# One DMA transpose for a unit's inner rows, and the last 32 rows by one TensorE transpose and one store

## The chip, the cores and the metric

The kernel runs on one core of a Trainium2 chip. The metric is the device time of one execution in microseconds (us); the time before is the median of three runs. Engines are named as the profile names them: PE is TensorE (PEld its weight loads), ACT is ScalarE, DVE is VectorE, POOL is GpSimd, SP is SyncE, which here only issues DMAs. "SPq", "ACTq" and "POOLq" are the instruction queues of those engines.

## The reference

A convolution over the sequence with three taps, a batch normalisation and SiLU, in bf16:

```python
B, S, C, K = 2, 2048, 1024, 3          # x: (B, S, C), w: (K, C, C)
xp = jnp.pad(x, ((0, 0), (1, 1), (0, 0)))
y = sum(jnp.einsum('bsc,cd->bsd', xp[:, k:k + S, :], w[k]) for k in range(K))
y = (y - mean) * (g / jnp.sqrt(var + 1e-5)) + b
return silu(y)
```

## The kernel before, in words

The three taps are done by a short-convolution transform: six neighbouring output positions (`R = 6`) form a block, and eight products (`NJ = 8`) give all six. 2048 positions make `NB = 342` blocks, of which the last holds only two real positions. `T_sb` holds the transformed input; the transformed weights `u` and a few untransformed ones (`wch`) are the stationary operands.

The work is cut into 16 units: `dc` (128 of the 1024 output channels) times `bi` (batch). Unit 14 is the last `dc` with batch 0, unit 15 the last `dc` with batch 1. A unit is 64 matmuls of 342 columns (8 products of 8 channel tiles, line 324), DVE combinations (line 342) and SiLUs on ACT (line 347). The SiLUs write `yT`, one tile for each batch, laid out as [channel, row i of the block, block]; the rows i go from 0 to 5. "Inner" rows are 1 to 4, "outer" ones 0 and 5. Then the data are turned to [block, row, channel] in a tile `o` and stored, so that each block's rows are rows of the output.

How the end of one unit lies inside the next: `Unit.run` takes a list of pairs (place, function) and calls the functions at the places 1 to 6 (`behind(n)`) of its own order of products. `rest` supplies three of them for the unit before: `silu_inner`, `last` (product 7 into row 5, then its SiLU) and `first` (product 0 into row 0, then its SiLU). During units 13 and 14 `silu_inner` and `last` stand at place 4 and `first` at place 5, between product (2,5) and product (2,6). The order on all engines is the program order; nothing is rearranged.

Units 0 to 13 are turned by a DMA transpose (`turn`, line 458), issued on SP after the next unit's `run`: one for all six rows, for unit 13 two (rows 1 to 5, row 0). They are stored one unit later by `store`: blocks 0 to 127, 128 to 255 and 256 to 335 (three DMAs, line 471), blocks 336 to 340 (one, line 471) and the two last positions (one, line 475). For units 12 and 13 the two small ones are issued on POOL (`late`).

Unit 15 is computed in two parts: `h0` (blocks 128 to 341) and `h1` (blocks 0 to 127). Unit 14 and unit 15 are turned on PE (`put`: transposes of 128x128 against `ident`, line 429, a copy out of PSUM, line 430, stores, line 435). Unit 14's inner rows of block groups 0 and 1 are put at place 5 of `h0.run` (8 transposes, a DVE copy), its outer rows at place 2 of `h1.run` (6 transposes, an ACT copy), its inner rows of group 2 at place 3 of `h1.run` (4 transposes, an ACT copy). `put_rest` stores its last six blocks with two DMAs on POOL (lines 446 and 450). Unit 15's stores go to SP and ACT, its `put_rest` to POOL.

Of the kernel before, what the change touches and what calls it, by code (L numbers as in the profile page):

```python
# [11 lines left out]
BF16 = mybir.dt.bfloat16  # L12
# [3 lines left out]
P = 128  # L16
R = 6
# [9 lines left out]
def kernel(  # L27
# [10 lines left out]
    nc = tc.nc  # L38
    B, S, C = x.shape
    D = w.shape[2]  # L40
    CT, DC = C // P, D // P
    NB = -(-S // R)
# [22 lines left out]
    ps = pspool.tile([P, 8, 512], FP32, name="ps")  # L65
    T_sb = [tpool.tile([P, CT, NJ, NB], BF16, name=f"T_sb{bi}") for bi in range(B)]

    rows = consts.tile([4 * DC, P], BF16, name="rows")
# [65 lines left out]
    def load_w(pair, k, half=None):  # L134

        if (pair, "tile") not in raw:
            raw[pair, "tile"] = wpools[pair % 2].tile([P, 3, CT, 2, P], BF16, name=f"wch{pair % 2}")
        wch = raw[pair, "tile"]
        h0, h1 = (0, 2) if half is None else (half, half + 1)
        cols = slice((2 * pair + h0) * P, (2 * pair + h1) * P)  # L140
        nc.sync.dma_start(  # L141
            out=wch[:, k, :, h0:h1].rearrange("p c h d -> p c (h d)"), in_=w_all[:, k, :, cols]
        )
        clock["dma"] += 1200.0 * (h1 - h0)
        for h in range(2):
            raw[2 * pair + h] = wch[:, :, :, h]
# [77 lines left out]
    ident = consts.tile([P, P], BF16, name="ident")  # L224
# [68 lines left out]
    NK = -(-NB // P)  # L293
    NBP = NK * P
    assert S % R
    yts = [ypool.tile([P, R, NBP], BF16, name=f"yT{q}") for q in range(B)]
    for t in yts:
        nc.gpsimd.memset(t[:, :, NB:NBP], 0.0)

    class Unit:  # L300
# [117 lines left out]

        def put(self, o, rows, bank, evac, queues, blocks=None):

            i0, i1 = min(rows), max(rows)
            every = slice(i0, i1 + 1, 1 if i1 == i0 else (i1 - i0) // (len(rows) - 1))
            blocks = blocks or range(self.lo // P, -(-self.hi // P))
            n = min(self.hi - self.lo, P)
            v = ps[:, bank].bitcast(BF16)[0:n, 0:len(rows) * len(blocks) * P]
            v = v.rearrange("p (i k d) -> p i k d", i=len(rows), k=len(blocks))
            for a, i in enumerate(rows):
                for q, k in enumerate(blocks):
                    nc.tensor.transpose(v[:, a, q], self.yT[:, i, k * P:k * P + n], ident)  # L429
            evac(o[0:n, every, blocks[0]:blocks[-1] + 1], v)  # L430
            outs = out[self.bi, :, self.dc * P:(self.dc + 1) * P]
            full = S // R
            for q, k in zip(queues, blocks):
                hi = min((k + 1) * P, full // 16 * 16)
                q.dma_start(
                    out=outs[k * P * R:hi * R].rearrange("(p i) d -> p i d", i=R)[:, every],
                    in_=o[0:hi - k * P, every, k],
                )

        def put_rest(self, o, queue):  # L440

            full = S // R
            lo = full // 16 * 16
            k, p0 = lo // P, lo % P
            rows = out[self.bi, :, self.dc * P:(self.dc + 1) * P]
            queue.dma_start(  # L446
                out=rows[lo * R:full * R].rearrange("(p i) d -> p i d", i=R), in_=o[p0:p0 + full - lo, :, k]
            )
            k, p0 = full // P, full % P
            queue.dma_start(  # L450
                out=rows[full * R:S].rearrange("(p i) d -> p i d", p=1), in_=o[p0:p0 + 1, 0:S % R, k]
            )

        def turn(self, pool=opool, parts=((0, R),)):

# [4 lines left out]
                    in_=self.yT[:, lo:hi].rearrange("d i (k p) -> d (i k) p", p=P),  # L460
                )

        def store(self, queues=()):

            o, full = self.o, S // R
            rows = out[self.bi, :, self.dc * P:(self.dc + 1) * P]
            cuts = [k * P for k in range(full // P + 1)] + [full // 16 * 16, full]
            queues = list(queues) or [nc.sync] * len(cuts)
            for q, lo, hi in zip(queues, cuts, cuts[1:]):
                k, p0 = lo // P, lo % P  # L470
                q.dma_start(
                    out=rows[lo * R:hi * R].rearrange("(p i) d -> p i d", i=R), in_=o[p0:p0 + hi - lo, :, k]
                )
            k, p0 = full // P, full % P
            queues[-1].dma_start(
                out=rows[full * R:S].rearrange("(p i) d -> p i d", p=1), in_=o[p0:p0 + 1, 0:S % R, k]
            )

    for i, wi in enumerate(order):
        load_x(0, wi)  # L480
# [22 lines left out]
    class Between:  # L503


        n = done = cols = 0
# [16 lines left out]

    between = Between()
    seq = [(dc, bi) for dc in range(DC) for bi in range(B)]
    late = [nc.sync] * (S // R // P + 1) + [nc.gpsimd]
    before = prev = None
    for i, (dc, bi) in enumerate(seq[:-1]):
        unit = Unit(dc, bi, i % 2 * 4)
        unit.run(  # L530
            between, prev.rest(between, *((4, 5) if i >= len(seq) - 3 else (5, 6))) if prev else [(5, between.rest)],
            1 if i == 0 else 2 if i == 2 else dc + 2 if bi == 1 and 0 < dc < DC - 2 else None,
        )
        if i == 0:
            xwin_scope.close()
            olast = ctx.enter_context(tc.tile_pool(name="olast", bufs=3))
            wpools[1] = ctx.enter_context(tc.tile_pool(name="wpool1", bufs=1))
        if i in (0, 4, 8):
            for k in range(3):
                load_w(i // 4 + 1, k)  # L540
        if i == len(seq) - 2:
            prev.turn(olast, ((1, R), (0, 1)))
        elif prev:
            prev.turn()
        if before:
            before.store(late if i == len(seq) - 2 else ())
        before, prev = prev, unit
    before.store(late)
    dc, bi = seq[-1]
    sp, ac = nc.sync, nc.scalar  # L550
    inner, outer = tuple(range(1, R - 1)), (0, R - 1)
    to_v, to_s = nc.vector.tensor_copy, nc.scalar.copy
    o = olast.tile([P, R, NK, P], BF16, name="o")
    h0 = Unit(dc, bi, 4, P, NB)
    h0.run(between, prev.rest(between, 5, 5) + [(5, lambda: prev.put(o, inner, 1, to_v, (sp, sp), (0, 1)))])
    h1 = Unit(dc, bi, 0, 0, P)
    h1.run(between, [
        (2, lambda: prev.put(o, outer, 2, to_s, (sp, sp, sp))),
        (3, lambda: prev.put(o, inner, 1, to_s, (sp,), (2,))), (3, lambda: prev.put_rest(o, nc.gpsimd)),
    ] + h0.rest(between, 5, 6))  # L560
    o2 = olast.tile([P, R, NK, P], BF16, name="o")
    h0.put(o2, inner, 5, to_v, (sp, sp))
# [2 lines left out]
    h1.last(between)  # L565
    h0.put(o2, outer, 6, to_v, (sp, ac))
    h1.put(o2, inner, 1, to_v, (ac,))
    h0.put_rest(o2, nc.gpsimd)
    h1.put(o2, outer, 2, to_v, (sp,))

_INS = ['x', 'w', 'mean', 'var', 'g', 'b']
# [25 lines left out]
```

## Time and profile before

| | |
|---|---|
| Median of 3 runs | 190.59 us (190.58 to 190.9) |
| The profiled execution's own time | 190.33 us |
| Its span | 188.5 us |
| Granted TensorE clock | 0.998 |
| PE busy | 177.7 us (94% of the span) |
| DVE, POOL, ACT busy | 155.5, 139.6, 111.2 us |
| DMA moved | 31.72 MB, mean 168 GB/s |
| DMAs issued on POOL | 8: four of 7.5 KB, four of 0.5 KB |

Times in the views are microseconds from the span's start. A timeline line reads: start, duration, engine, line of the kernel, operation, out<-in, shape, number of instructions merged, and in brackets the idle time before and who ended it. In the tables by stretch the columns are the length, then busy time and number of instructions of PE, PEld, DVE, ACT and POOL, the granted clock, the busy share of the DMA engines and GB/s. Matmuls overlap in their pipeline, so starts, not ends, tell PE's pace.

### The profile page before, as it was taken

To read this page: it belongs to the slowest core of one execution; us is meant where nothing else is said; L and a number is where in the kernel's file an instruction comes from. 1 tells how busy PE (TensorE), PEld (TensorE's weight loads), DVE (VectorE), ACT (ScalarE), POOL (GpSimd) and SP (SyncE) were. 2 spreads that over 40 slices of the span, in tenths; PEclk is the share of its full clock that TensorE was granted. 3 is DMA by queue.
4 is the path that set the end of the run, shared out by engine and by line. 5 is a ranking of instruction groups with operands and counts; after the bars stand their busy time and mean duration, and the time that the engine had idled before them with its cause. 6 is when DMAs were issued, how large, how long until landed. Compare 5 with 4: busy or idle time off the path is not lost.

```text
span 188.5 us, 3727 instructions
## 1 busy us (share of the span) xinstructions
PE 177.7 (94%) x1404; PEld 125.7 (67%) x1404; DVE 155.5 (82%) x214; ACT 111.2 (59%) x181; POOL 139.6 (74%) x83
## 2 busy tenths in 40 slices
PE   7777799999999999999999999999999999999990
PEld 3665688766666666666666666666666666669980
DVE  5546887989989899988898899879979996769680
ACT  3777887875456565365635554555455555454790
POOL 3445999976797889999999999799999772021022
PEclk9999999999999999999999999999999999999999
DMA  5999999065245938599659586997595677979735
GB/s 172 332 311 360 384 378 211 2 197 144 50 76 31 202 74 171 145 221 209 124 117 203 112 157 180 193 201 151 117 208 112 129 85 155 178 139 170 157 65 108
DMA packets 86958, 31.72 MB, mean 168 GB/s; under 512 B 73542, under 2 KB 82778, under 8 KB 86940
## 3 DMA queue, kind: packets, MB, share of 16 engines
q1 hardware_dynamic: 85916, 31.27, 74.6%
q10 hardware_dynamic: 768, 0.18, 0.5%
q8 instruction: 11, 0.18, 0.4%
q0 software_dynamic: 256, 0.03, 0.2%
q14 instruction: 7, 0.06, 0.1%
HBM read 14.82 MB, written 8.39 MB: 123 GB/s over the span
## 4 chain that ended last, share of the span: by engine, by line
PE 84%; DMA 6%; DVE 4%; SPq 2%; issue 1%; POOL 0%; POOLq 0%; DVEq 0%
PE ps L324 78%; DMA xw<-in_x_dram 6%; PE ps L278 5%; DVE T_sb L291 4%; SPq L125 1%; PE ps L429 1%; POOL out_dram L446 0%; POOLq L592 0%; DVE o L430 0%; SPq L141 0%; DVEq L291 0%
## 5 line engine op out<-in xcount | busy, mean ns | idle before, releaser
L324 PE MATMUL ps<-T_sb,u 128*128 128x342 bf16 (+2 forms) x816 | 120.9, 299 | 0.2 <-ACT T_sb L289 0.2
L324 PEld LDWEIGHTS <-u 128*128 128x128 bf16 x816 | 76.8, 97 | 33.4 <-issue 0.2
L190 POOL TENSOR_TENSOR u<-e,w1x 128x1024 bf16<-128x1024 f32 x32 | 70.3, 2220 | 9.4 <-DVE e L171 9.3
L324 PE MATMUL ps<-T_sb,wch 128*128 128x342 bf16 (+2 forms) x272 | 42.5, 299 | 0.0
L347 ACT ACTIVATE yT<-ps,beta,scale 128x342 bf16<-128x342 f32 (+5 forms) x51 | 34.0, 703 | 11.8 <-PE ps L324 11.8
L342 DVE SCALAR_TENSOR_TENSOR t<-ps,sd 128x684 f32<-128x684 f32 (+2 forms) x51 | 39.1, 821 | 0.6
L190 POOL TENSOR_TENSOR u<-e,wch 128x1024 bf16<-128x1024 f32 x16 | 36.6, 2308 | 1.7 <-DMA wch<-in_w_dram 1.1
L324 PEld LDWEIGHTS <-wch 128*128 128x128 bf16 x272 | 25.7, 97 | 11.5
L335 ACT COPY pc<-ps 128x342 f32<-128x342 f32 (+2 forms) x34 | 14.5, 425 | 31.7 <-PE ps L324 30.9
L291 DVE CAST T_sb<-ps 128x1008 bf16<-128x1008 f32 (+2 forms) x20 | 21.6, 1104 | 10.8 <-PE ps L278 10.6
L278 PE MATMUL ps<-rm,xw 128*128 128x168 bf16 (+2 forms) x272 | 26.0, 240 | 4.6 <-DMA xw<-in_x_dram 3.3
L289 ACT CAST T_sb<-ps 128x1008 bf16<-128x1008 f32 (+2 forms) x30 | 25.1, 873 | 6.5 <-PE ps L278 6.4
L342 DVE SCALAR_TENSOR_TENSOR ps<-ps,t 128x684 f32<-128x684 f32 (+2 forms) x34 | 28.3, 831 | 0.6
L171 DVE SCALAR_TENSOR_TENSOR e<-wch 128x1024 f32<-128x1024 bf16 x14 | 28.6, 2045 | 0.0
L278 PEld LDWEIGHTS <-xw 128*128 128x128 bf16 (+2 forms) x272 | 21.3, 101 | 9.8 <-DMA xw<-in_x_dram 4.7
L342 DVE SCALAR_TENSOR_TENSOR ps<-ps,pc 128x342 f32<-128x342 f32 (+2 forms) x34 | 16.9, 497 | 8.7 <-PE ps L324 5.7
L169 POOL TENSOR_TENSOR e<-wch 128x1024 f32<-128x1024 bf16 x8 | 19.0, 2370 | 3.9 <-DMA wch<-in_w_dram 2.4
L347 ACT ACTIVATE yT<-t,beta,scale 128x684 bf16<-128x684 f32 (+2 forms) x17 | 15.7, 926 | 0.0
L342 DVE SCALAR_TENSOR_TENSOR t<-ps,t 128x684 f32<-128x684 f32 (+2 forms) x17 | 13.9, 817 | 0.0
L337 ACT ACTIVATE pc<-ps 128x342 f32<-128x342 f32 (+2 forms) x17 | 7.5, 440 | 9.8 <-PE ps L324 6.0
L335 ACT COPY sd<-ps 128x342 f32<-128x342 f32 (+2 forms) x17 | 7.3, 429 | 10.1 <-PE ps L324 9.7
L342 DVE SCALAR_TENSOR_TENSOR sd<-pc,ps 128x342 f32<-128x342 f32 (+2 forms) x17 | 8.3, 486 | 5.5 <-ACT sd L335 5.4
(46 smaller groups left out, 42.7 us busy)
## 6 DMA issues: line engine op xcount, KB each, us to landing
xw<-in_x_dram SPq DMA_DIRECT2D x32, 256.0 KB
out_dram<-o SPq DMA_DIRECT2D x28, 192.0 KB
wch<-in_w_dram SPq DMA_DIRECT2D x9, 512.0 KB
out_dram<-o SPq DMA_DIRECT2D x14, 120.0 KB
wch<-in_w_dram SPq DMA_DIRECT2D x6, 256.0 KB
out_dram<-o SPq DMA_DIRECT2D x3, 128.0 KB
out_dram<-o SPq DMA_DIRECT2D x4, 64.0 KB
o<-yT SPq DMA_TRANSPOSE x15
```

The source lines that it names most:

```text
L125: nc.sync.dma_start(out=xw[0:hi - lo, :], in_=x[bi, lo:hi, :])
L169: eng.tensor_tensor(e, w0, w2, op=ALU.add)
L171: eng.scalar_tensor_tensor(out=e, in0=f, scalar=4.0, in1=h, op0=ALU.mult, op1=ALU.add)
L190: nc.gpsimd.tensor_tensor(wts[dc, q][:, i], sums[dc, q], o, op=(ALU.add, ALU.subtract)[i])
L278: nc.tensor.matmul(v[:, q, c], lhsT=xw[0:rows, (c0 + c) * P:(c0 + c + 1) * P], rhs=mat[0:rows, :, 0:n], start=True, stop=True,)
L289: nc.scalar.copy(dst, src)
L291: nc.vector.tensor_copy(dst, src)
L324: nc.tensor.matmul(self.bank[q], lhsT=lhsT, rhs=T_sb[self.bi][:, ct, j, nsl], start=not add and ct == 0, stop=ct == CT - 1, skip_group_che ...
L335: nc.scalar.copy(dst, self.bank[q])
L337: nc.scalar.mul(dst, self.bank[q], by)
L342: nc.vector.scalar_tensor_tensor(out=out, in0=in0, scalar=scalar, in1=in1, op0=ALU.mult, op1=op1)
L347: nc.scalar.activation(self.yT[:, rows, self.lo:self.hi], src, ACT.Silu, bias=beta[:, dc:dc + 1], scale=scale[:, dc:dc + 1])
```

## The change

- `put_rest` is now a computation. POOL copies the last 6 blocks of all six rows of `yT` into a small tile `y` of 36 columns in output order; PE transposes it (one matmul); ACT copies 32 rows of the result to `o_rest`; `send_rest` stores them with one DMA of 32 rows of 256 B. It holds for units 12 to 15.
- For units 12 and 13 it is called at place 5 of the next unit's `run`, behind `first`; its DMA goes to SP, after the three stores of `store`. POOL issues no DMA any more.
- Unit 14's inner rows, all three block groups, go through one DMA transpose on SP, issued at place 5 of `h0.run`, ahead of `last` and `first`. The 8 and the 4 transposes with their copies are gone. Its outer rows stay on PE; its inner stores (three DMAs on SP) come at place 3 of `h1.run`, then the DMA of its rest.
- Unit 15's rest is transposed after its other copies but one, copied by ACT and stored from ACT's queue.

```diff
+    REST = S // R // 16 * 16          # 336
...
-        def put_rest(self, o, queue):
-            ...
+        def put_rest(self, bank, evac):
+            n = (NB - REST) * R
+            v = ps[0:n, bank].bitcast(BF16)[:, 0:P]
+            y = rpool.tile([P, n], BF16, name="y")
+            nc.gpsimd.tensor_copy(
+                y.rearrange("d (t i) -> d t i", i=R), self.yT[:, :, REST:NB].rearrange("d i t -> d t i")
+            )
+            nc.tensor.transpose(v, y, ident)
+            n = S - REST * R
+            self.o_rest = rpool.tile([n, P], BF16, name="rest")
+            evac(self.o_rest, v[0:n])
+
+        def send_rest(self, queue):
+            queue.dma_start(out=out[self.bi, REST * R:S, self.dc * P:(self.dc + 1) * P], in_=self.o_rest)
...
-        def store(self, queues=()):
+        def store(self, rest=True):
...
+            parts = [k * P for k in range(full // P + 1)] + ([REST, full] if rest else [REST])
...
+            else:
+                self.send_rest(nc.sync)
...
-    late = [nc.sync] * (S // R // P + 1) + [nc.gpsimd]
     before = prev = None
     for i, (dc, bi) in enumerate(seq[:-1]):
         unit = Unit(dc, bi, i % 2 * 4)
+        also = prev.rest(between, *((4, 5) if i >= len(seq) - 3 else (5, 6))) if prev else [(5, between.rest)]
+        if i >= len(seq) - 3:
+            also.append((5, lambda u=prev: u.put_rest(u.b0 + 1, nc.scalar.copy)))
         unit.run(
-            between, prev.rest(between, *((4, 5) if i >= len(seq) - 3 else (5, 6))) if prev else [(5, between.rest)],
+            between, also,
...
+            rpool = ctx.enter_context(tc.tile_pool(name="rpool", bufs=4))
...
         if before:
-            before.store(late if i == len(seq) - 2 else ())
+            before.store(i < len(seq) - 2)
         before, prev = prev, unit
-    before.store(late)
+    before.store(False)
...
-    o = olast.tile([P, R, NK, P], BF16, name="o")
     h0 = Unit(dc, bi, 4, P, NB)
-    h0.run(between, prev.rest(between, 5, 5) + [(5, lambda: prev.put(o, inner, 1, to_v, (sp, sp), (0, 1)))])
+    ready, *others = prev.rest(between, 5, 5)
+    h0.run(between, [ready, (5, lambda: prev.turn(olast, ((1, R - 1),)))] + others)
     h1 = Unit(dc, bi, 0, 0, P)
     h1.run(between, [
-        (2, lambda: prev.put(o, outer, 2, to_s, (sp, sp, sp))),
-        (3, lambda: prev.put(o, inner, 1, to_s, (sp,), (2,))), (3, lambda: prev.put_rest(o, nc.gpsimd)),
+        (2, lambda: prev.put(prev.o, outer, 2, to_s, (sp, sp, sp))), (3, lambda: prev.put_rest(1, to_s)),
+        (3, lambda: prev.send(prev.o, inner, (sp, sp, sp), range(NK))), (3, lambda: prev.send_rest(sp)),
     ] + h0.rest(between, 5, 6))
...
     h1.put(o2, inner, 1, to_v, (ac,))
-    h0.put_rest(o2, nc.gpsimd)
+    h0.put_rest(7, to_s)
+    h0.send_rest(ac)
     h1.put(o2, outer, 2, to_v, (sp,))
```

`send` is the tail of the old `put` (the stores) as a function of its own.

More of the change, by code (lines that the diff above doesn't have):

```diff
@@ L295, with every @@
     assert S % R
+    REST = S // R // 16 * 16
+    def every(rows):
+        i0, i1 = min(rows), max(rows)
+        return slice(i0, i1 + 1, (i1 - i0) // (len(rows) - 1))
     yts = [ypool.tile([P, R, NBP], BF16, name=f"yT{q}") for q in range(B)]
@@ L419, in put @@
         def put(self, o, rows, bank, evac, queues, blocks=None):
-            i0, i1 = min(rows), max(rows)
-            every = slice(i0, i1 + 1, 1 if i1 == i0 else (i1 - i0) // (len(rows) - 1))
             blocks = blocks or range(self.lo // P, -(-self.hi // P))
@@ L429, in put, with send @@
                     nc.tensor.transpose(v[:, a, q], self.yT[:, i, k * P:k * P + n], ident)
-            evac(o[0:n, every, blocks[0]:blocks[-1] + 1], v)
+            evac(o[0:n, every(rows), blocks[0]:blocks[-1] + 1], v)
+            self.send(o, rows, queues, blocks)
+        def send(self, o, rows, queues, blocks):
             outs = out[self.bi, :, self.dc * P:(self.dc + 1) * P]
-            full = S // R
             for q, k in zip(queues, blocks):
-                hi = min((k + 1) * P, full // 16 * 16)
+                hi = min((k + 1) * P, REST)
                 q.dma_start(
-                    out=outs[k * P * R:hi * R].rearrange("(p i) d -> p i d", i=R)[:, every],
-                    in_=o[0:hi - k * P, every, k],
-                )
-        def put_rest(self, o, queue):
[L442 to L447, printed above, removed]
-            )
[L449 to L452, printed above, removed]
+                    out=outs[k * P * R:hi * R].rearrange("(p i) d -> p i d", i=R)[:, every(rows)],
+                    in_=o[0:hi - k * P, every(rows), k],
+                )
+        def put_rest(self, bank, evac):
[4 more added lines that the diff above has]
+                y.rearrange("d (t i) -> d t i", i=R), self.yT[:, :, REST:NB].rearrange("d i t -> d t i")
+            )
+            nc.tensor.transpose(v, y, ident)
[4 more added lines that the diff above has]
+            queue.dma_start(out=out[self.bi, REST * R:S, self.dc * P:(self.dc + 1) * P], in_=self.o_rest)
         def turn(self, pool=opool, parts=((0, R),)):
@@ L461, in turn @@
                 )
-        def store(self, queues=()):
+        def store(self, rest=True):
             o, full = self.o, S // R
             rows = out[self.bi, :, self.dc * P:(self.dc + 1) * P]
-            cuts = [k * P for k in range(full // P + 1)] + [full // 16 * 16, full]
-            queues = list(queues) or [nc.sync] * len(cuts)
-            for q, lo, hi in zip(queues, cuts, cuts[1:]):
+            parts = [k * P for k in range(full // P + 1)] + ([REST, full] if rest else [REST])
+            for lo, hi in zip(parts, parts[1:]):
                 k, p0 = lo // P, lo % P
-                q.dma_start(
+                nc.sync.dma_start(
                     out=rows[lo * R:hi * R].rearrange("(p i) d -> p i d", i=R), in_=o[p0:p0 + hi - lo, :, k]
                 )
[L474 to L477, printed above, removed]
+            if rest:
+                k, p0 = full // P, full % P
+                nc.sync.dma_start(
+                    out=rows[full * R:S].rearrange("(p i) d -> p i d", p=1), in_=o[p0:p0 + 1, 0:S % R, k]
+                )
+            else:
+                self.send_rest(nc.sync)
     for i, wi in enumerate(order):
```

## The prediction, as put on record

> **What bounds the kernel now.** I read the page first, for the engine that fills the span and the chain that ended last:
>
> ```profile
> PE 177.7 (94%) x1404; PEld 125.7 (67%) x1404; DVE 155.5 (82%) x214; ACT 111.2 (59%) x181; POOL 139.6 (74%) x83
> ...
> PE 84%; DMA 6%; DVE 4%; SPq 2%; issue 1%; POOL 0%; POOLq 0%; DVEq 0%
> PE ps L324 78%; DMA xw<-in_x_dram 6%; PE ps L278 5%; DVE T_sb L291 4%; SPq L125 1%; PE ps L429 1%; POOL out_dram L446 0%; POOLq L592 0%; DVE o L430 0%; SPq L141 0%; DVEq L291 0%
> ```
>
> TensorE carries 84% of the chain, and POOL's last store closes it. A mean says nothing about the place of the edit, so the table by stretch comes next, around the end of units 11 to 14 and at the tail:
>
> ```profile
> 160.00:162.00 2.00, 2.00 (x15) 1.34 (x14) 1.72 (x3) 0.44 (x1) 0.00 (x0) 1.00 0.60 112
> ...
> 168.00:170.00 2.00, 2.00 (x18) 1.56 (x17) 0.46 (x1) 0.64 (x1) 0.00 (x0) 1.00 1.15 213
> ...
> 182.00:184.00 2.00, 1.73 (x22) 1.16 (x19) 1.63 (x5) 1.56 (x4) 0.24 (x1) 1.00 0.19 38
> 184.00:186.00 2.00, 0.00 (x0) 0.00 (x0) 0.17 (x1) 0.00 (x0) 0.87 (x2) 1.00 0.98 194
> 186.00:188.50 2.50, 0.00 (x0) 0.00 (x0) 0.00 (x0) 0.00 (x0) 0.00 (x0) 0.86 0.13 27
> ```
>
> Until 183.8 PE is never free, POOL is idle, and the last 2.5 us of data are limited by the DMA engines (0.98 of them busy). Then the timeline, for the exact place at which the new step is called:
>
> ```profile
> 157.66 1.32 PE L324 MATMUL ps<-T_sb,wch 128*128 128x342 bf16 x8
> ...
> 158.82 5.97 PE L324 MATMUL ps<-T_sb,u 128*128 128x342 bf16 x40
> 159.02 0.64 ACT L347 ACTIVATE yT<-ps,beta,scale 128x342 bf16<-128x342 f32 x1 [0.66 <-PE ps L324]
> 159.68 2.75 SPq L458 DMA_TRANSPOSE o<-yT  x1
> ...
> 166.65 3.54 SPq L458 DMA_TRANSPOSE o<-yT  x2
> ```
>
> The 8 matmuls on `wch` at 157.66 are `first`; the next product starts at 158.82 without a gap; the SiLU of row 0 runs beside it and ends at 159.66. The same figure stands in the next unit at 166.95, 168.10 and 168.31. The starts are 0.145 us apart (5.80 us for 40), and 342 columns at 0.145 us leave no room for catching up. Last, the chain at the end:
>
> ```profile
> 175.42 0.45 PE ps L429 x8
> 175.87 1.63 PE ps L324 x24
> 177.50 0.34 PE ps L429 x6
> 177.84 0.45 PE ps L324 x8
> 178.28 0.22 PE ps L429 x4
> 178.50 2.81 PE ps L324 x40
> ...
> 183.76 0.59 POOL out_dram L446
> 184.35 0.51 POOLq L592
> ```
>
> **Part 1, the rest of units 12 and 13: two waits on TensorE.** `put_rest` is called straight behind `first`. Its POOL copy reads all six rows, row 0 too, so it can't start before that SiLU ends; the PE transpose waits for the copy; and behind it in PE's queue stands product (2,6), which needs neither. What was a SiLU beside matmuls becomes a chain of four engines with PE standing still. From the row at 157.66: PE would go on at 158.82. The SiLU ends at 159.66. From ACT to POOL takes 0.07 to 0.10 us (a copy on ACT, L239, ends at 6.72, POOL's L246 behind it starts at 6.82); from POOL to a waiting PE 0.06 us to the weight load and 0.07 more to the matmul (a POOL result at 32.60, weight load 32.66, matmul 32.73); the transpose takes its slot of 0.055 us (8 in 0.45). The POOL copy of 36 elements in each partition isn't in the trace. Its bounds are the shortest POOL row, 0.10 us (a memset of 8 elements), and 1.04 us for 1024 elements in bf16 (L178). The operations on 8 elements take 0.19 to 0.21 us, one on 128 elements 0.35, so I take 0.22. PE goes on at 159.66 + 0.10 + 0.22 + 0.13 + 0.055 = 160.16: 1.34 us late. Two units: **+2.68 us**; by the bounds of the copy +2.4 to +4.3. Below 0.84 us for one wait (SiLU's end less 158.82) it can't go, as the queue is in order. A gap as long (1.24 us, ended by a DMA at 16.09) left the granted clock at 1.00 in the trace, so I add nothing for slower matmuls. Behind PE also wait the copies on ACT and combinations on DVE of that unit; they only move along. The ACT copy of 32 rows falls into ACT's idle time.
>
> **Part 2, unit 14's inner rows: transposes leave PE.** 8 + 4 transposes go (0.45 + 0.22 us of the chain), one comes (0.055): **-0.61 us**, all on the chain. A DVE copy (0.69 us) and an ACT copy (0.61) go with them, beside PE; DVE's 0.20 us wait for that ACT copy at 179.36 goes too, so DVE moves ahead by as much as PE and does not become the next bound. Unit 14's and unit 15's small POOL copies have POOL to themselves and are done before PE asks.
>
> **Part 3, the moved DMAs on SP.** From unit 12's stores on SP gains seven issues (three rests, one transpose, three inner stores) and loses the three of L435 that they replace. The three stores of unit 12 were issued by 172.56, those of unit 13 by 174.80; one wait of 1.34 us later that is 173.9 and 176.1, and each rest store (about 0.42 us, as L435's) follows there, while the transpose of unit 14 can't start before its inner SiLUs end (175.15 + 2.68 = 177.8): free. That transpose has 12 of 128x128 where unit 12's had 18 (issued 159.68, POOL's store behind it released at 164.59: 4.9 us) and unit 13's 15 + 3 (166.65, its first store at 172.84: 6.2 us). So it lands at 182.7 to 184.0, and PE stands 2.07 us late by then: 180.7 to 182.0 on the clock of the trace before. Behind it SP issues three inner stores and the rest, 4 x 0.45 = 1.8 us: until 182.5 to 183.8. Unit 15's first store was issued at 182.74, so it is between 0 and 1.1 us late. Its data ran into busy DMA engines and nothing later hides that; I take **+0.3 us** and keep 0 and 1.1.
>
> **Part 4, the very end.** POOL's two stores go; unit 15's rest store is issued on ACT after an ACT copy (about 0.27 us, as the 128-column copies) behind the store that ended at 184.36, so by 185.05. The trace has POOL's last store issued by 184.87 and landed at 187.07, SP's last 184.73 and 186.94: the same 2.2 us, so landing is worth nothing either way. But after the last landing SP walks through nine waits on pairs of semaphores, 187.09 to 187.61; eight of the 18 semaphores are POOL's DMAs. Without them there are five waits: 4 x 0.062 = **-0.25 us**.
>
> A rule of the Trainium skill stands beside the row on landing. "DMA: Bandwidth & Descriptors", section "Latency and other measured facts", gives some 0.6 us to the first byte for DMAs from SP or ACT and about 1 us for those from GpSimd. By it the end would gain a further 0.4 us (an estimate from that page), and the forecast would be 192.3; the two stores issued side by side at the end show no such difference, and I go by them. The same page, section "Issuing engines are not separate DMA queues", speaks against moving stores to SP for bandwidth: all queues share 16 engines, so only issue time moves.
>
> **The sum.** +2.68 - 0.61 + 0.3 - 0.25 = +2.12 us. On the profiled execution, 190.33 (span 188.5 and 1.8 around it), that is 192.45; the median of the runs is 0.26 higher, 190.59, and gives **192.7**.
>
> **Rivals.**
> - *Unit 14's transpose sets the end.* For it: unit 13's two pieces took 6.2 us, eight DMA semaphores serve all stores in turn, so unit 15's last stores need unit 14's inner ones landed. Against: 4.9 us for a larger one. Price: 1.1 instead of 0.3, or a little more: 193.5 to 194. Chance 0.15.
> - *The POOL copy is slow* (two-byte elements picked from six rows, after 3 us of idleness): near the 1.04 us row, +1.64 for both: 194.3. Against: the rows for 8 and 128 elements. Chance 0.06.
> - *Faster: the waits cost PE nothing net*, because the chain leaves PE: if from unit 13 on DVE or the DMA queue were what everything waits for, PE's standing still would take the place of waits it has later anyway, and only the other terms stay. With the +0.3 that is 190.0. It decides from a net cost of 0.28 us for each wait, (0.61 + 0.25 - 0.3) / 2, downward. Against: 2.00 of 2.00 in every stretch from 160, and only one short wait of PE at the end (0.13 us, at 182.17). Chance 0.05.
> - *The change does not do what it says*: the POOL copy of unit 15's rest waits for `h1`'s SiLUs too, if writes to other columns of `yT` count as a conflict; then the last PE transposes come about 0.5 us later: 193.2. Against: an ACT copy into rows 0 and 5 of `o` at 177.87 did not wait for the stores of rows 1 to 4 issued at 176.70. Chance 0.02, inside the range.
>
> **How the numbers follow.** The forecast has 0.72. Its own terms give +1.5 (copy at 0.10 us, SP not late, the end 0.1 better) to +2.9 (SP 1.1 late): 192.1 to 193.5. With the transpose rival the range reaches 194.2; below it I go down to 191.7, for waits 0.15 us shorter each than the hops add up to. No change means within 0.2%, 0.38 us, about what a measurement of this kernel can tell: that needs the waits to cost 0.09 to 0.47 us each (2 w - 0.56 within 0.38), which the 0.84 us floor excludes unless PE has slack unseen here. Faster 0.05, same 0.03, slower 0.92.
>
> **What would show it.** Right: two gaps of PE of about 1.3 us behind `first` of units 12 and 13, ended by POOL's `y`, and every later start 2.7 us late until 178; `y` copies of about 0.2 us; PE's last matmul near 185.9; SP's first store for unit 15 within half a microsecond of its DVE copy; five closing waits on SP. Wrong: no PE gap there or one under 0.8 us; PE catching up before the tail; SP waiting for unit 14's transpose past the time when unit 15's first copy is done.

## The result, and the profile after

The changed kernel takes 193.24 us, the median of four runs (193.19 to 193.38); the kernel before had 190.59 beside it. The ratio is 1.0144, with an interval of 1.0119 to 1.0169: 2.65 us slower where +2.12 was forecast. The profiled execution took 193.38 us, its span is 191.6.

Four lines of the page of the changed kernel, which is organised like the page before (in the last one: number of instructions, then busy time and mean ns of one, then idle time before them and who ended it):

```profile
PE 177.7 (93%) x1396; PEld 124.3 (65%) x1396; DVE 155.0 (81%) x213; ACT 111.6 (58%) x184; POOL 135.8 (71%) x79
...
q8 instruction: 11, 0.18, 0.4%
...
PE 84%; DMA 6%; DVE 4%; SPq 2%; ACT 1%; issue 1%; POOL 0%; ACTq 0%; DVEq 0%
...
L452 POOL COPY y<-yT 128x36 bf16<-128x36 bf16 x4 | 1.0, 240 | 26.8 <-ACT yT L353 26.8
```

PE is busy for as long as before, 177.7 us, with eight instructions fewer; the span is longer by 3.1. ACT has come into the chain with 1%. The new POOL copy takes 240 ns. The queue of instruction fetches (`q8`, 11 transfers) will matter below.

The table by stretch shows where PE stands still. Columns as before: length, busy time and count of PE, PEld, DVE, ACT, POOL, granted clock, DMA share, GB/s; the lower rows are of 1 us each:

```profile
158.00:160.00 2.00, 1.37 (x10) 0.68 (x7) 0.97 (x2) 1.04 (x2) 0.00 (x0) 1.00 0.71 141
160.00:162.00 2.00, 1.61 (x11) 1.07 (x12) 0.00 (x1) 0.30 (x2) 0.24 (x1) 1.00 0.27 51
...
170.00:172.00 2.00, 0.97 (x8) 0.65 (x8) 0.00 (x0) 0.89 (x2) 0.24 (x1) 1.00 1.15 211
...
185.00:186.00 1.00, 1.00 (x17) 0.80 (x15) 0.67 (x2) 1.00 (x4) 0.00 (x0) 1.00 0.77 155
186.00:187.00 1.00, 0.56 (x4) 0.24 (x3) 0.85 (x3) 0.28 (x1) 0.00 (x0) 1.00 0.06 8
187.00:188.00 1.00, 0.00 (x0) 0.00 (x0) 0.00 (x0) 0.26 (x1) 0.00 (x0) 1.00 0.59 124
```

Stretches that were full (2.00 of 2.00) now lack about 1 us of PE at two places, at an unchanged clock of 1.00: the first is split over two rows (0.63 and 0.39), the second lies in one (1.03). DVE falls to 0.00 at both, as it waits for PE. And at 186 to 187 us, where unit 15's stores should be under way, the DMA engines are at 0.06.

The timeline at the two places (start, duration, engine; the brackets name the idle time and who ended it):

```profile
158.04 1.32 PE L330 MATMUL ps<-T_sb,wch 128*128 128x342 bf16 x8
159.41 0.64 ACT L353 ACTIVATE yT<-ps,beta,scale 128x342 bf16<-128x342 f32 x1 [0.66 <-PE ps L330]
160.10 0.24 POOL L452 COPY y<-yT 128x36 bf16<-128x36 bf16 x1 [2.96 <-ACT yT L353]
160.39 0.23 PE L455 MATMUL ps<-ident,y 128*36 128x128 bf16 x1 [1.03 <-POOL y L452]
160.56 5.98 PE L330 MATMUL ps<-T_sb,u 128*128 128x342 bf16 x40
...
168.70 1.32 PE L330 MATMUL ps<-T_sb,wch 128*128 128x342 bf16 x8
171.04 0.23 PE L455 MATMUL ps<-ident,y 128*36 128x128 bf16 x1 [1.03 <-POOL y L452]
171.21 1.04 PE L330 MATMUL ps<-T_sb,u 128*128 128x342 bf16 x6
```

The chain of four engines can be read off: `first` on PE, SiLU on ACT, copy on POOL, transpose on PE. Eight matmuls at 0.145 us would have let the next product start at 158.04 + 1.16 = 159.20; it started at 160.56, 1.36 us late. The second time it is 171.21 instead of 169.86: 1.35.

To put the other terms beside this, I split both spans from the start of unit 12's first product, which lies ahead of everything that the change touches (from the records of instructions and of DMA landings):

| us | before | after | difference |
|---|---|---|---|
| start of unit 12's first product | 143.69 | 144.05 | +0.36 |
| from there to PE's last transpose | 39.92 | 42.28 | **+2.36** |
| from it to the end of the last DVE copy | 0.56 | 0.56 | 0 |
| from that copy to the last landing | 2.90 | 3.74 | **+0.84** |
| from the last landing to the end | 1.41 | 0.99 | **-0.42** |

The three terms in bold sum to +2.78. The first row is the input part, the same program in both; it differs from one execution to the next and is why the two profiled spans stand further apart than the medians.

### The profile page after: what moved, and what is told of

Same layout as the page of the kernel before. It is cut to its first block, busy times and chain, and to the rows that moved or that the text cites. A ratio compares the mean times of both kernels' runs of the same rounds, so it can differ in the third digit from the quotient of the medians.

```text
span 191.6 us, 3710 instructions
## 1 busy us (share of the span) xinstructions
PE 177.7 (93%) x1396; PEld 124.3 (65%) x1396; DVE 155.0 (81%) x213; ACT 111.6 (58%) x184; POOL 135.8 (71%) x79
## 4 chain that ended last, share of the span: by engine, by line
PE 84%; DMA 6%; DVE 4%; SPq 2%; ACT 1%; issue 1%; POOL 0%; ACTq 0%; DVEq 0%
PE ps L330 77%; DMA xw<-in_x_dram 6%; PE ps L278 5%; DVE T_sb L291 4%; SPq L125 1%; PE ps L433 1%; ACT yT L353 1%; PE ps L455 0%; POOL y L452 0%; SPq L141 0%; DVE o L434 0%; ACT rest L458 0%; ACTq L442 0%; DVEq L291 0%
## 5 line engine op out<-in xcount | busy, mean ns | idle before, releaser
L278 PE MATMUL ps<-rm,xw 128*128 128x168 bf16 (+2 forms) x272 | 25.5, 234 | 5.4 <-DMA xw<-in_x_dram 4.3
L278 PEld LDWEIGHTS <-xw 128*128 128x128 bf16 (+2 forms) x272 | 20.3, 98 | 11.3 <-DMA xw<-in_x_dram 6.3
L452 POOL COPY y<-yT 128x36 bf16<-128x36 bf16 x4 | 1.0, 240 | 26.8 <-ACT yT L353 26.8
```

What stands on the lines that cost most here:

```text
L278: nc.tensor.matmul(v[:, q, c], lhsT=xw[0:rows, (c0 + c) * P:(c0 + c + 1) * P], rhs=mat[0:rows, :, 0:n], start=True, stop=True,)
```

## The experiments

Times are medians; the kernel before ran beside each of them. Three questions: do the two waits carry the loss, is the tail worth anything by itself, and why are unit 15's stores late on SP?

### The same step one place later

```diff
-            also.append((5, lambda u=prev: u.put_rest(u.b0 + 1, nc.scalar.copy)))
+            also.append((6, lambda u=prev: u.put_rest(u.b0 + 1, nc.scalar.copy)))
```

> The change with one thing moved: the rests of units 12 and 13 are put at place 6 (behind product (2,6)) instead of place 5. PE then has 8 matmuls of 342 columns (1.16 us) in front of the transpose while SiLU and POOL copy run, out of the 1.36 us that each wait costs now. Theory (each wait is paid in full by the end): two waits of about 0.2 us stay, 2.3 us are gained: 190.9 us, +0.3 on the kernel before. Rival (PE's standing still is given back elsewhere, and the loss comes from the tail alone): 193.2 us as with the change.

191.0 us against 190.57, ratio 1.0026 (1.0012 to 1.0039). The timeline at the first of the two places:

```profile
158.31 1.32 PE L330 MATMUL ps<-T_sb,wch 128*128 128x342 bf16 x8
...
159.47 1.32 PE L330 MATMUL ps<-T_sb,u 128*128 128x342 bf16 x8
159.67 0.64 ACT L353 ACTIVATE yT<-ps,beta,scale 128x342 bf16<-128x342 f32 x1 [0.66 <-PE ps L330]
160.37 0.24 POOL L452 COPY y<-yT 128x36 bf16<-128x36 bf16 x1 [3.11 <-ACT yT L353]
...
160.72 0.23 PE L455 MATMUL ps<-ident,y 128*36 128x128 bf16 x1
160.89 4.82 PE L330 MATMUL ps<-T_sb,u 128*128 128x342 bf16 x32
```

The 8 matmuls of product (2,6), 1.16 us, now run behind `first` (158.31) while ACT and POOL do the SiLU and the copy; `y` is done at 160.61, just before PE is through with them at 160.63. What stays is the transpose itself with the change to it and back: the next product starts at 160.89, 0.26 us late, and 0.26 at the second place too. PE's last transpose comes 40.02 us after unit 12's first product, 2.26 less than in the changed kernel. So nearly all that the change costs hangs on this one place, and not on the POOL copies. The 0.52 us that stay are more than PE gains in the tail (0.42, by the tail-only kernels below), so this kernel is no gain over the one before either.

### The rests of units 12 and 13 alone

The tail as before, POOL's two-store rest for units 14 and 15 included; of the change only these lines and the functions that they call are kept:

```diff
+        if i >= len(seq) - 3:
+            also.append((5, lambda u=prev: u.put_rest(u.b0 + 1, nc.scalar.copy)))
...
-            before.store(late if i == len(seq) - 2 else ())
+            before.store(i < len(seq) - 2)
...
-    before.store(late)
+    before.store(False)
```

> The kernel before with one part of the change: the rests of units 12 and 13 by POOL copy, PE transpose, ACT copy and one store on SP, at place 5. Units 14 and 15 as before. Theory: +2.7 us from two waits of 1.36, less 0.1 for four semaphores fewer at the close: 193.2 us. Rival (loss in the tail): 190.6 us.

193.36 us against 190.57, ratio 1.015 (1.0132 to 1.0168). The chain:

```profile
159.49 0.65 ACT yT L353
...
160.19 0.24 POOL y L452
...
160.47 0.23 PE ps L455
160.71 9.41 PE ps L330 x64
```

The same detour over ACT and POOL, without the tail's change. PE's last transpose comes 42.62 after unit 12's first product: +2.70 against before. This part alone costs as much as the whole change, so the rest of the change is worth nothing, or gains what it loses.

### The tail alone, twice

The change without the step at place 5; units 12 and 13 store their rests from POOL as before:

```diff
-        if i >= len(seq) - 3:
-            also.append((5, lambda u=prev: u.put_rest(u.b0 + 1, nc.scalar.copy)))
...
-                self.send_rest(nc.sync)
+                # two stores of the old put_rest
+                self.put_rest_two(o, nc.gpsimd)
```

> The kernel before with the other part: units 14 and 15 as in the change, the small stores of units 12 and 13 on POOL as before. Theory: the change less its two waits, 193.2 - 2.7 = 190.5 us, the 0.61 us taken off PE being lost again because SP, held in the issue of unit 14's rest store for 1.8 us, sends unit 15's first store about 1.3 us after its copy. Rival (loss in the tail): 193.2 us. If SP isn't held here: 189.5 us or less.

> The tail-only kernel once more beside it, since its gain (ratio 0.9986) was no larger than its interval. Theory by the terms measured: PE 0.42 and closing 0.24 us earlier, stores 0.33 us later, together -0.33 us: a ratio of 0.998. Rival (its last stores are held by the fetch in most runs): 1.000 to 1.003.

190.53 us against 190.57, ratio 0.9986 (0.997 to 1.0001); the second time 190.82 against 190.49, ratio 1.0013 (0.9993 to 1.0032). Both intervals hold 1: no difference. Yet PE's last transpose comes 39.50 and 39.49 after unit 12's first product, 0.42 earlier than before, in both. The gain on PE is real and does not reach the end. SP's own timeline in the first of them tells where it goes (instructions of one line are merged):

```profile
175.45 2.11 SPq L481 DMA_TRANSPOSE o<-yT  x1
178.53 3.05 SPq L442 DMA_DIRECT2D out_dram<-o  x6
182.02 0.35 SPq L475 DMA_DIRECT2D out_dram<-rest  x1
182.61 3.02 SPq L442 DMA_DIRECT2D out_dram<-o  x4
```

SP takes up unit 15's four stores on time, 0.03 us behind the DVE copy, but needs 3.02 us for them where the kernel before needed 1.99 for its four (182.74 to 184.73). The first of the four alone took 1.01 us, and SP's last store starts 0.74 us behind its DVE copy (1.00 in the repeat, 0.12 before). From the last DVE copy to the last landing it is 3.23 and 3.44 us, against 2.90.

### Unit 14's inner transpose alone

The kernel before with the DMA transpose of unit 14's inner rows, its three inner stores on SP, and the rests of all units as before on POOL:

```diff
-    h0.run(between, prev.rest(between, 5, 5) + [(5, lambda: prev.put(o, inner, 1, to_v, (sp, sp), (0, 1)))])
+    ready, *others = prev.rest(between, 5, 5)
+    h0.run(between, [ready, (5, lambda: prev.turn(olast, ((1, R - 1),)))] + others)
...
-        (3, lambda: prev.put(o, inner, 1, to_s, (sp,), (2,))), ...
+        (3, lambda: prev.send(prev.o, inner, (sp, sp, sp), range(NK))), ...
```

> The kernel before with one part of the change: unit 14's inner rows by one DMA transpose and three stores on SP. All rests as before, two POOL stores each. PE loses 12 transposes, 0.66 us by their slots. Theory (SP has only one issue more and the transpose ahead of unit 15's stores, so little of it is lost again): the last landing 2.9 to 3.3 us behind the last copy, 190.2 us (190.0 to 190.4) against 190.6. Rival (the data of the inner rows, 0.34 MB some 4 us later than before, fill the end whatever SP does): 3.5 us or more, 190.6 us.

190.78 us against 190.75, ratio 1.0004 (0.9977 to 1.003). PE is 0.54 us earlier at its last transpose (39.38), and all of it is lost again. SP's stores by line (min/median/max of the duration in ns):

```profile
L441 SPq DMA_DIRECT2D out_dram<-o x10: 372/485/1537, 179.6 to 186.3; - x10
```

Ten stores, half of them under 0.485 us, and one of 1.537, issued at 182.25 us: without the rest's transposes, too, one issue is three times as long as the others, and SP is 1.37 us late for unit 15's first store. The last landing is 3.89 us behind the last copy, the rival's number, but not for its reason: SP's last store began 2.00 us behind that copy and landed 1.90 after its start (0.12 and 2.64 in the kernel before).

### What makes one issue long: PE's program moved

In the changed kernel the long one is the store of unit 14's rest. SP's timeline there:

```profile
184.21 0.53 SPq L442 DMA_DIRECT2D out_dram<-o  x1
184.84 1.83 SPq L461 DMA_DIRECT2D out_dram<-rest  x1
186.72 2.17 SPq L442 DMA_DIRECT2D out_dram<-o  x4
```

1.83 us for 8 KB; the same store took 0.63 us for units 12 and 13. Unit 15's first copy is done at 185.42. With an issue of 0.63 SP would have been free at 185.47, 0.05 late; it came at 186.72, 1.30 late. The trace's DMA records show one 16 KB instruction fetch at 184.78, 1.49 us long. If that fetch is the cause, the long issue must move when PE's program is moved against its fetches, and if it is this store's form, it must stay. Two kernels try it, the whole change in both:

```diff
# first: more and narrower warm-up matmuls
-    for _ in range(WARM):
-        nc.tensor.matmul(ps[:, 7], lhsT=zeros[:, 0:P], rhs=zeros, start=True, stop=True)
+    for _ in range(WARM * 5):
+        nc.tensor.matmul(ps[:, 7, 0:104], lhsT=zeros[:, 0:P], rhs=zeros[:, 0:104], start=True, stop=True)
# second: 24 small matmuls in gaps of the input part
+        for _ in range(pad):    # 6 at each of four places
+            nc.tensor.matmul(src[:, 0, 0:32], lhsT=zeros[:, 0:P], rhs=zeros[:, 0:32], start=True, stop=True)
```

> The change with 24 more pairs of weight load and matmul in PE's warm-up (30 of 104 columns instead of 6 of 512), so that PE reaches its last fetch of instructions (16 KB, at 184.78 in the trace of the change, 1.49 us) 24 pairs sooner, near 183.1. Theory (a fetch holds one DMA engine, and SP's issue waits for that engine): the long issue of 1.8 us moves to one of unit 14's inner stores at 183.2 to 184.7, the rest store takes 0.4 to 0.6, SP reaches unit 15's first store 0.5 to 1.2 us earlier, and the time falls to 192.3 (192.0 to 192.8), if the longer warm-up costs nothing. Rival (this store's own issue is slow, behind full queues): the rest store still takes 1.8 us and the time stays at 193.2.

> The change with the same 24 small matmuls in the waits for x, where the longer warm-up of the earlier run cost 1.7 us at the start. Theory (SP's long issue comes of the fetch beside it): the last landing is 3.1 to 3.2 us behind the last copy instead of 3.74, and the time 192.6 us (192.4 to 192.9). Rival (no fetch effect): 193.2 us.

193.66 us against 190.57, ratio 1.0139 (1.0114 to 1.0163), and 193.64 against 190.65, ratio 1.0156 (1.0126 to 1.0186). Neither time is a gain over the change, and both missed their forecasts (192.3 and 192.6). In both profiled executions, the slowest of their runs, unit 12's first product started late, at 145.74 and 145.48 instead of 144.05, so the times can't be set side by side with the change's; only the places can. SP in the second:

```profile
182.74 5.09 SPq L444 DMA_DIRECT2D out_dram<-o  x6
187.94 0.42 SPq L463 DMA_DIRECT2D out_dram<-rest  x1
188.40 2.09 SPq L444 DMA_DIRECT2D out_dram<-o  x4
```

The rest's store takes 0.42 us now: its form is not what made it long. The six stores of unit 14 ahead of it took 5.09 us, because one of them, issued at 183.70, took 2.19; and the fetch lies at 183.91 in this kernel, 1.59 us long. So the long issue moved with the fetch here, onto another store of the same queue, and SP was later than in the changed kernel (1.61 us); that is why the time forecast for it failed. In the first kernel, where the fetch lies at 184.08, the long issue is gone instead: the two stores beside the fetch take 0.47 and 0.68 us and the rest's store 0.42, SP comes 0.33 us late instead of 1.30, and the last landing is 3.15 us behind the last copy instead of 3.74. So the long issue did not belong to the rest's store, and a fetch does not always make one.

The tail alone with the same 24 matmuls:

> The tail-only kernel (units 14 and 15 as in the change, units 12 and 13 as before) with the 24 small PE matmuls in the waits for x, so that PE's last fetch comes about 1.7 us sooner, among unit 14's inner stores, behind which SP has some 0.5 us to spare before unit 15's first store. Theory: the last landing 2.9 to 3.0 us behind the last copy instead of 3.23; if the small matmuls cost nothing at the start 190.2 us, 0.2% under the kernel before. Rival (SP is held as long and keeps the delay to the end): 3.2 us or more, 190.5 us or more.

190.82 us against 190.49, ratio 1.0009 (0.9983 to 1.0036). The fetch came at 179.84 and the store issued at 179.67 took 1.52 us, onto the outer stores of unit 14 again; SP was 0.91 late for unit 15. The time is no better than with the fetch at 182.31: SP's queue handed the delay on to unit 15's stores.

### POOL's part of the tail

*Without any DMA on POOL,* the kernel before otherwise:

```diff
-    late = [nc.sync] * (S // R // P + 1) + [nc.gpsimd]
...
-            before.store(late if i == len(seq) - 2 else ())
+            before.store()
...
-        ... (3, lambda: prev.put_rest(o, nc.gpsimd)),
+        ... (3, lambda: prev.put_rest(o, sp)),
...
-    h0.put_rest(o2, nc.gpsimd)
+    h0.put_rest(o2, ac)
```

> The kernel before with its eight POOL stores moved, nothing else: units 12 to 14 to SP, unit 15 to ACT's queue. It measures the closing term alone. In the trace of before the end lies 1.41 us behind the last landing, in that of the change 0.99. Theory (SP walks through the semaphores of all DMA queues in use): 0.99 again, and the time falls by 0.4 us to 190.15. Rival (the saving belonged to something else of the change, or later landings eat it): 190.6 us.

191.36 us against 190.65, ratio 1.004 (1.0023 to 1.0057). From the last landing to the end it is 0.96 us, 0.45 less than before: POOL's DMAs do cost that at the close. But SP:

```profile
179.07 3.96 SPq L435 DMA_DIRECT2D out_dram<-o  x6
183.08 0.83 SPq L446 DMA_DIRECT2D out_dram<-o  x1
183.96 0.64 SPq L450 DMA_DIRECT2D out_dram<-o  x1
184.70 2.16 SPq L435 DMA_DIRECT2D out_dram<-o  x4
```

Two small stores (7.5 and 0.5 KB) take 0.83 and 0.64 us to issue and stand ahead of unit 15's, whose first copy was done at 183.32: 1.38 late; without these two SP would have been free at 183.04. More is lost than the close gains.

*Unit 14's inner stores and rest on POOL instead of SP,* on the tail-only kernel:

```diff
-        (3, lambda: prev.send(prev.o, inner, (sp, sp, sp), range(NK))), (3, lambda: prev.send_rest(sp)),
+        (3, lambda: prev.send(prev.o, inner, (nc.gpsimd,) * 3, range(NK))), (3, lambda: prev.send_rest(nc.gpsimd)),
```

> The kernel of the tail-only run (190.53 us) with unit 14's three inner stores and its rest store issued on POOL instead of SP. There the last landing is 3.23 us behind the last copy, against 2.90 before. Theory (SP's queue, with 4 more issues ahead of unit 15's stores and held during a fetch, sends the last stores late): 2.9 again, 190.2 us. Rival (the data of unit 14's inner rows, moved nearer to the end, fill the DMA engines whoever issues them): 3.2 again, 190.5 us.

191.06 us against 190.65, ratio 1.0029 (1.0012 to 1.0046). SP is on time, first store and last (0.03 us). The experiment brought in a wait of its own, though: unit 15's `y` copy stands behind POOL's issues. The timeline:

```profile
184.37 0.25 POOL L452 COPY y<-yT 128x36 bf16<-128x36 bf16 x1
184.68 0.23 PE L455 MATMUL ps<-ident,y 128*36 128x128 bf16 x1 [1.09 <-POOL y L452]
```

PE waits 1.09 us for it. That is a fault of the design, so the time is no answer, and the next kernel has no such copy. The landing is an answer in part: with SP on time the last landing is still 3.56 us behind the last copy, as SP's last store landed 3.53 after its start (2.64 before). That speaks for the rival.

*Unit 14's inner transpose alone, its inner stores on POOL,* all rests as before:

> As the kernel with the inner transpose alone, with the three inner stores on POOL instead of SP; here no POOL copy stands behind them on PE's way. Theory (SP is what loses the gain): 0.1 to 0.3 us faster than that kernel, 190.0 us. Rival (data at the end): no faster, or slower, since POOL's stores carry the same bytes: 190.3 us or more.

191.58 us against 190.75, ratio 1.003 (1.0007 to 1.0052). SP is on time here (0.03 late at first, 0.50 at last) and PE 0.54 earlier, and it is slower still, with 4.92 us from the last DVE copy to the last landing. The table by stretch:

```profile
182.00:184.00 2.00, 1.17 (x14) 0.68 (x11) 1.25 (x4) 1.01 (x3) 2.00 (x5) 1.00 0.80 179
184.00:186.00 2.00, 0.00 (x0) 0.00 (x0) 0.00 (x0) 0.00 (x0) 1.10 (x3) 1.00 0.91 167
```

POOL's issuing fills 2.00 of 2.00 us, and unit 14's data now run in the same stretch as unit 15's, with the DMA engines at 0.80 and 0.91. SP's last store landed 4.05 us after its start, and POOL's last, which began at 184.58, closes the data. Freeing SP only moved the queue into the data. Over these kernels the two trade: where SP's last store began late (1.57 us in the changed kernel, 2.00 with the inner transpose alone) it landed 2.17 and 1.90 after its start; with unit 14's inner stores on POOL SP was nearly on time and it took 3.53 and 4.05. Only in the changed kernel with the longer warm-up, whose inner stores met no long issue on SP, were both small (0.46 and 2.69), and that is one execution.

*The tail alone, no DMA on POOL for units 12 and 13, and the 24 matmuls:*

```diff
-                self.put_rest_two(o, nc.gpsimd)
+                self.put_rest_two(o, nc.sync)
```

> The tail-only kernel, without POOL stores (units 12 and 13 store their small pieces on SP) and with 24 extra small PE matmuls laid into waits for x in the first 17 us, so that the last fetch of PE's instructions falls about 2.4 us sooner. By the terms measured so far: PE 0.42 us earlier, closing 0.42 us shorter, the stores 0 to 0.3 late: 189.9 us (189.7 to 190.2), faster than both kernels. Rival (fetch and closing play no part): 190.5 us as the tail-only kernel.

191.91 us against 190.65, ratio 1.006 (1.0042 to 1.0077): slower, where 189.9 was forecast. SP:

```profile
176.63 0.84 SPq L468 DMA_DIRECT2D out_dram<-o  x1
177.51 0.63 SPq L472 DMA_DIRECT2D out_dram<-o  x1
178.27 1.47 SPq L483 DMA_TRANSPOSE o<-yT  x1
179.84 5.06 SPq L444 DMA_DIRECT2D out_dram<-o  x6
```

Unit 13's two small stores hold unit 14's transpose back until 178.27 (175.45 in the tail-only kernel), SP stands from 182.34 to 183.39 ahead of the first of the stores that need it, and comes 2.58 us late to unit 15's. This is the rival of the prediction in which unit 14's transpose sets the end; it occurs here, not in the changed kernel.

No kernel of these beats the one before.

## Why the prediction was right

**The two waits, +2.68: shown.** 1.36 and 1.35 us in the trace against 1.34, the POOL copy 0.24 against 0.22. That the total fits so closely is luck in part: the hops took 0.06 and 0.05 us where I had 0.10 and 0.13, and the transpose held PE for 0.16 where I had one slot of 0.055, and the two errors cancel. The kernel with this part alone gives +2.70 on PE and a ratio of 1.015, and one place later all but 0.26 us of each goes. PE did not catch up, and the clock stayed at 1.00 behind the gaps.

**Transposes off PE, -0.61: the right sign, a third too much.** The tail-only kernels have -0.42, the inner transpose alone -0.54. The mis-sized step is "all on the chain" for the four transposes of block group 2. The chain from the end of the outer transposes to the next transposes, first in the changed kernel, then with the inner transpose alone:

```profile
180.50 0.45 PE ps L330 x8
180.95 0.16 PE ps L455
181.11 2.92 PE ps L330 x40
184.03 0.45 PE ps L433 x8
```

```profile
178.07 3.41 PE ps L324 x48
181.48 0.45 PE ps L429 x8
```

In the kernel before this stretch took 3.47 us (177.84 to 181.31, four transposes of 0.22 among its 48 matmuls). Without them it takes 3.41, so 0.06 came back and not 0.22: at 178.96 PE now waits 0.16 us for ACT's copy of the outer rows, a wait that the four transposes had filled. With the transpose of unit 14's rest in that place it takes 3.53. So the first eight transposes gave their 0.45, the other four with what replaced them cost 0.06, and -0.39 is left, near the -0.42. Unit 15's rest, which I did not count, costs PE nothing: from the first of unit 15's last 18 transposes to the last it takes 2.31 us before (181.31 to 183.62) and 2.30 with the rest's among them (184.03 to 186.33), because the last ones wait for ACT's SiLUs in any case. I had read only one short wait at PE's end, at 182.17; the trace before has three more, of 0.08 to 0.29 us, at 182.92, 183.27 and 183.62.

**SP late, +0.3: measured +0.84, inside its bounds of 0 and 1.1, and for another reason.** I bounded it by unit 14's DMA transpose, which was to land at 182.7 to 184.0. It landed by 182.14, 3.68 us after its issue where I had 4.9 to 6.2, so this bound did not act. The step that failed is "4 x 0.45" for the three inner stores and the rest: they took 0.37, 0.50, 0.53 and 1.84 us. The mark that I had set, SP's first store for unit 15 within half a microsecond of its copy, was missed (1.30). SP's last store began 1.57 us behind its DVE copy where it was 0.12 before, 1.45 more; it landed 2.17 us after the start of its issue instead of 2.64, and POOL's store, which landed 0.13 after SP's in the kernel before, is gone: 1.45 - 0.47 - 0.13 = 0.85.

**The close, -0.25: measured -0.42.** SP's waits by line in the changed kernel, with those of its rest stores (number, then min/median/max ns):

```profile
L607 SPq EVENT_SEMAPHORE  x7: 17/28/28, 189.1 to 191.6; - x7
...
L461 SPq DMA_DIRECT2D out_dram<-rest x3: 628/635/1835, 175.0 to 184.8; - x3
```

Seven where the kernel before has eleven: the four that I counted are gone. The first comes at 189.1, ahead of the last landing at 190.63, and so does the second; only three of the waits on DMAs lie behind that landing, where the kernel before has all nine. Six fewer at 0.062 us are 0.37 of the 0.42. The forecast left out that waits can lie beside data under way. So the close goes by the waits that are left, not by the number of POOL's DMAs alone: it takes 0.96 to 0.99 us with none of them, 1.17 to 1.20 with four, but with eight 1.41 in the kernel before and 1.17 and 1.23 in two kernels in which SP's last landing came later than POOL's.

**The rivals.** A slow POOL copy: no, 0.24 us. A false wait of unit 15's copy on `yT`: no, it ran at 184.7 and PE took its result at 185.96 without waiting. The waits costing nothing net: no, +2.70 on PE came out at the end as +2.8 on the time when alone (193.36 less 190.57). The forecast came out 0.5 too low (2.12 against 2.65 by the medians) because two errors, of +0.19 on the transposes and +0.54 on SP, had one sign, and the close gave back 0.17. So the direction and most of the size come from the two waits, whose mechanism is shown; that the SP term fell inside its bounds is luck, since its reason was another.

The rule of the Trainium skill that all queues share the same DMA engines ("DMA: Bandwidth & Descriptors", section "Issuing engines are not separate DMA queues") goes on to say that issuing from several engines saves only issue time, usually small beside the transfer. The first half agrees with the kernel whose inner stores were on POOL, where the DMA engines were 0.91 busy and nothing was won. The second did not fit this kernel's end when POOL's stores were moved: two of 7.5 and 0.5 KB kept SP for 0.83 and 0.64 us, of 2.08 and 1.74 from the start of their issue to landing, and the kernel with all eight moved to SP and ACT has a ratio of 1.004.

## What to carry to other kernels

Before a step of several engines is put into the queue of the engine that is the bound, find the work behind it there that does not need its result: put the step behind at least as much of that work as the chain is long (here 1.16 us of matmuls, one place further on, hid the 1.14 us of SiLU and copy; of two waits of 1.36 us 0.26 each was left, the transpose itself, and 2.26 us came back). At the end of a kernel, time saved on the computing engine is worth only what the issuing queue passes on, so write out that queue's issues with their durations and look for room between them before counting the gain.

## What the runs showed of the hardware that was not expected

**A DMA issue on SP that lies beside an instruction fetch can take 1.0 to 2.2 us.** Each of these programs has 11 fetches of 16 KB on one queue. Over the fourteen profiled executions shown here, 20 of SP's stores took 0.97 us or more to issue, and 19 of them overlap a fetch in time; the other, of 1.10 us, came directly behind a DMA transpose, and of all the rest that overlap no fetch none exceeds 0.90. The reverse does not hold: of 48 stores that overlap a fetch 29 took less, 22 of them under 0.70 us. The last fetches, against the longest of SP's stores beside them, by the DMA records and the instructions' times, first where an issue was long, then where none was:

| kernel | fetch starts, us | its length | the issue starts | its length |
|---|---|---|---|---|
| changed | 184.78 | 1.49 | 184.84 | 1.84 |
| changed, 24 matmuls in the gaps | 183.91 | 1.59 | 183.70 | 2.19 |
| inner transpose alone | 182.15 | 1.24 | 182.25 | 1.54 |
| tail alone, 24 matmuls more | 179.84 | 0.95 | 179.67 | 1.52 |
| tail alone | 182.31 | 0.93 | 182.61 | 1.01 |
| tail alone, again | 182.52 | 1.12 | 182.82 | 1.21 |
| one place later | 183.42 | 0.92 | 183.63 | 1.08 |
| no DMA on POOL | 181.71 | 0.93 | 181.97 | 1.06 |
| changed, longer warm-up | 184.08 | 1.13 | 184.87 | 0.68 |
| tail alone, inner stores and rest on POOL | 182.27 | 1.25 | 183.42 | 0.53 |
| inner transpose alone, stores on POOL | 181.43 | 1.06 | 182.18 | 0.38 |
| tail alone, none on POOL, 24 matmuls | 180.97 | 0.89 | 181.59 | 0.67 |

In the kernel before the fetch came at 181.01 and was over by 182.18; SP issued nothing from 180.64 to 182.74, and no issue of its tail exceeds 0.50 us; with the rests of units 12 and 13 alone the fetch came at 184.19, and SP issued nothing from 184.10 to 185.94. That the fetch moves with PE's program, and that long issues occur beside fetches (19 of 48) and hardly elsewhere (1 of 1038), is shown. When a fetch makes an issue long and how it holds it is not: in the changed kernel 15 of the 16 landings of each of the two stores issued before it came by 185.96 and 186.29 and the last one at 187.54 and 187.76, while the DMA engines were at 0.06. This would fit one engine that is held up by the fetch and an issue that waits for room on it, but no run here separates that from other causes.

**The duration of an issue does not go with the bytes.** On SP, away from fetches, a store of 2 rows (0.5 KB) takes 0.63 to 0.67 us, one of 5 blocks (7.5 KB) 0.83 to 0.90, one of 32 rows (8 KB) 0.35 to 0.64, one of 128 KB 0.37 to 0.63 and once 0.85. Merging a rest's two stores into one saves issues, then, and not transfer.
